# Twenty-four two-element memsets at the head of GpSimd's program and twenty-four behind VectorE's constants

## The chip, the cores and the metric

The kernel runs on one core of one Trainium2 chip. The metric is device time in microseconds (us), the median of the runs; lower is better. The core has five engines that run their own instruction streams in order: TensorE (PE, with its weight loads PEld), VectorE (DVE), ScalarE (ACT), GpSimd (POOL) and SyncE (SP, which here only issues DMAs). Semaphores order work between them.

## The reference

A sliding-window attention with four sink tokens, and behind it a channel mix of the RWKV kind. Inputs are float32; q, k and v have the shape (4, 8, 768, 64), d_model is 512 and d_ff is 1024.

```python
scores = scale * np.matmul(q, k.transpose(0, 1, 3, 2))
keep = (pos[None, :] < n_sink) | ((rel >= 0) & (rel < window))   # n_sink 4, window 128
a = softmax(np.where(keep, scores, -1e9))
x = (a @ v) as (batch, seq, heads * head_dim)

x_prev = x shifted by one position, zeros first
xk = mu_k * x + (1 - mu_k) * x_prev
xr = mu_r * x + (1 - mu_r) * x_prev
k = np.maximum(xk @ w_k, 0.0)
out = sigmoid(xr @ w_r) * (k * k @ w_v)
```

## The kernel before, in words

The work is cut into twelve units: four batches times three stretches of 256 positions. A unit is loaded (q, k and v by SP's DMA queue, line 337 for k and q, line 307 for v), prepared (casts to bf16 at line 543 and 646, transposes on PE at line 576, copies out of PSUM at line 589), attended (scores at line 721, exponentials on ACT at line 775, the product with v at line 808, division by the sum at lines 822 and 825), mixed (transposes at line 849, difference at line 877, the two mixtures at line 888) and sent through the channel mix (products at lines 939, 979 and 997, which use weights cast to bf16).

The order is written out by hand. Every step is an operation of a plan, and the tuple `ORDER` lists all of them in one sequence; negative numbers in it are filler matmuls, products of the zero tile `warm` that keep PE occupied (line 1018). `P.run()` emits the operations in that sequence, so that each engine's own stream is the subsequence that belongs to it. Each engine waits in order: a filler behind a waiting instruction waits too. The framework adds the semaphore waits that data dependencies ask for.

What stands at the beginning matters here. The program begins with an entry part of the framework (shown as line 1056), in which GpSimd sets four constants of one element per partition, and a barrier of all engines. Then:

- VectorE sets `warm` (line 1038), then `ones`, `spread` and `hmask` (line 402, function `fill`), then the sink tiles, the ones column of the v tiles and the first columns of the x tiles (lines 408, 410 and 412, function `fill_later`). Its next instruction is the first cast of k (line 543), which waits for a DMA.
- GpSimd makes the 128 x 128 identity from `ones` in two selects (line 418), an 8 x 8 float32 copy of it, `ident8` (line 424), then four selects for `hmask`, five selects and a memset for the two bias tiles (`bias0` and `bias1`, in a tile that the profile calls `ob`), two copies for `spread` (line 451), and then its first cast of q (line 543), which waits for a DMA.
- PE runs six fillers on `warm`, then `spread_mu` (line 486), a transpose of the mixing factors that reads `ident8` and the factors that two DMAs on ACT's queue bring (line 374), then seven more fillers, then the first transposes of k (line 576, they read the identity), then four matmuls that put the bias into PSUM (line 728, they read `bias0` and the identity), and so on.

```python
    def spread_mu():
        nc.tensor.transpose(out=buf["mup"][:, 0:2 * NC], in_=rows8, identity=ident8)
...
    with tc.manual_schedule():
        nc.vector.memset(warm, 0.0)
        P.run()
```

Of the kernel before, what the change touches and what calls it, by code (L numbers as in the profile page):

```python
# [9 lines left out]
BF16 = mybir.dt.bfloat16  # L10
# [175 lines left out]
def kernel(  # L186
# [14 lines left out]
    nc = tc.nc  # L201
# [45 lines left out]
    def tile1(shape, dtype, name):  # L247
        return const.tile(shape, dtype, name=name)
# [129 lines left out]
    def const_op(engine, cost, emit, writes=(), reads=(), rank=-50):  # L378
        P.op(engine, cost, emit, rank, writes=writes, reads=reads, port=engine == "POOL")
# [17 lines left out]
    xts = [tile1([128, NC, S + 16], BF16, f"xt{i}") for i in range(2)]  # L397
    ones = tile1([128, 128], BF16, "ones")

    def fill():  # L400
        for t, value in ((ones, 1.0), (spread, 0.0), (hmask, 1.0)):
            nc.vector.memset(t, value)
        if VS:
            nc.vector.memset(pick, 0.0)

    def fill_later():
        for t in ksink + vsink:
            nc.vector.memset(t, 0.0)
        for t in P.pools["vb"]:
            nc.vector.memset(t[:, :, :, D:D + 1], 1.0)  # L410
        for t in xts:
            nc.vector.memset(t[:, :, 0:16], 0.0)

    const_op("DVE", 500.0, fill, ["ones0"], rank=-80)
    const_op("DVE", 1800.0, fill_later, ["sinks0", "ones", "edges"], rank=-79)

    def keep(out, base, pattern, multiplier, in_=ones, fill=0.0):
        nc.gpsimd.affine_select(out=out, in_=in_, compare_op=ALU.is_ge, fill=fill, base=base,
                                pattern=pattern, channel_multiplier=multiplier)
# [6 lines left out]
    def window_mask(out, in_, fill):  # L426
        keep(out[:, 0:128], -1, [[-1, 128]], 1, in_, fill)
        keep(out[:, 128:256], 0, [[1, 128]], -1, in_, fill)
# [607 lines left out]
    ffn(U - 1, 10 * U + FFN_AFTER)  # L1036
    with tc.manual_schedule():
        nc.vector.memset(warm, 0.0)  # L1038
        P.run()


# [33 lines left out]
```

## Time and profile before

| what | value |
|---|---|
| median of 3 runs | 166.21 us (166.19 to 166.28) |
| span of the profiled execution, first to last instruction | 164.3 us |
| what lies around the span, against the median | 1.9 us |
| PE busy | 158.4 us (96%) |
| VectorE busy | 145.4 us (89%) |
| ScalarE busy | 131.2 us (80%) |
| GpSimd busy | 13.5 us (8%), 38 instructions |

The profile comes from one execution, and the records give no device time of their own for it beside its span; the median of the runs is 1.9 us above that span. All starts below are counted from the span's begin. In a row of a timeline the first number is the start, the second the time until the end of the last instruction that the row merges, "x4" the number of them, and the bracket says how long the engine had been idle and what released it. A shape such as 128x512 is partitions by elements of each. The page has a row for the granted clock of TensorE, in tenths of full speed.

### The profile page before, as it was taken

The numbers are of one execution on the slowest core, as the hardware profiler recorded it, in microseconds if no ns is written. First come the engines' busy times: TensorE is split into PE (matmuls) and PEld (weight loads), VectorE is DVE, ScalarE is ACT, GpSimd is POOL, SyncE is SP. The second block draws the span as 40 slices with busy tenths as digits, with TensorE's granted clock in tenths as the row PEclk, the third lists the DMA queues.
The fourth block names the chain that finished last, engine by engine and source line by source line (L and its number), as shares of the span: only waits on it lengthen the run. The fifth ranks groups of instructions, "written<-read, shape, count | busy, mean of one in ns | idle before, by whom it ended". The sixth has DMA issues, their size and how long they took to land.

```text
span 164.3 us, 4195 instructions
## 1 busy us (share of the span) xinstructions
PE 158.4 (96%) x1603; PEld 102.6 (62%) x1603; DVE 145.4 (89%) x381; ACT 131.2 (80%) x218; POOL 13.5 (8%) x38
## 2 busy tenths in 40 slices
PE   6999889999999999999999999999999999999992
PEld 2455568866467587577566775856575765664851
DVE  5259999999999999989999999999999999789752
ACT  3277999999999999999999999997668759163240
POOL 6409300010000000060000000000000000000000
PEclk9999999999999999999999999999999999999999
DMA  4999999999969896999999887986996955077743
GB/s 120 247 305 311 348 335 355 301 354 210 228 154 270 135 240 148 234 198 167 224 216 157 188 156 163 235 146 150 199 123 136 362 149 200 0 90 297 262 185 128
DMA packets 79042, 34.60 MB, mean 211 GB/s; under 512 B 67112, under 2 KB 73520, under 8 KB 79024
## 3 DMA queue, kind: packets, MB, share of 16 engines
q1 hardware_dynamic: 79008, 34.35, 86.3%
q8 instruction: 12, 0.20, 0.6%
q14 instruction: 6, 0.05, 0.1%
q10 hardware_dynamic: 16, 0.00, 0.0%
HBM read 24.12 MB, written 6.29 MB: 185 GB/s over the span
## 4 chain that ended last, share of the span: by engine, by line
PE 79%; ACT 8%; SPq 4%; DMA 3%; issue 2%; DVE 1%; POOL 1%; DVEq 0%; ACTq 0%; POOLq 0%
PE bank L997 23%; PE bank L939 23%; PE bank L979 12%; PE bank L808 6%; PE sc L721 6%; SPq L337 3%; DMA qs<-in_q_dram 3%; PE bank L576 2%; ACT e L775 2%; PE bank L849 2%; ACT rl L949 1%; PE bank L763 1%; ACT qt L589 1%; PE bank L909 1%; PE bank L1018 1%
## 5 line engine op out<-in xcount | busy, mean ns | idle before, releaser
L775 ACT ACTIVATE e<-sc 128x1024 bf16<-128x1024 f32 (+1 forms) x48 | 46.1, 994 | 1.8 <-PE sc L721 1.7
L939 PE MATMUL bank<-xk,wk_sb 128*128 128x256 bf16 x384 | 47.1, 273 | 0.0
L997 PE MATMUL bank<-wv_h,kk 128*128 128x512 bf16 x184 | 43.1, 379 | 0.1
L939 PEld LDWEIGHTS <-wk_sb 128*128 128x128 bf16 x384 | 36.4, 98 | 7.4 <-issue 0.4
L949 ACT ACTIVATE rl<-bank 128x512 bf16<-128x512 f32 x40 | 24.2, 625 | 8.6 <-PE bank L939 7.1
L997 PEld LDWEIGHTS <-kk 128*128 128x128 bf16 x184 | 17.1, 98 | 17.8 <-issue 0.4
L789 DVE TENSOR_TENSOR e<-e,mask 128x1024 bf16<-128x1024 bf16 (+1 forms) x40 | 25.4, 642 | 0.7 <-ACT e L775 0.5
L979 PE MATMUL bank<-wr_sb,xr 128*128 128x512 bf16 x96 | 23.7, 379 | 0.0
L888 DVE SCALAR_TENSOR_TENSOR xk<-td,mu_all,xt 128x256 bf16<-128x256 bf16 x48 | 22.4, 483 | 0.3
L888 DVE SCALAR_TENSOR_TENSOR xr<-td,mu_all,xt 128x256 bf16<-128x256 bf16 x48 | 22.1, 475 | 0.2
L967 ACT ACTIVATE kk<-rl 128x512 bf16<-128x512 bf16 x29 | 18.3, 664 | 4.2 <-DVE rl L953 4.0
L985 ACT ACTIVATE th<-bank 128x512 f32<-128x512 f32 x24 | 15.1, 646 | 5.7 <-PE bank L979 5.7
L825 DVE TENSOR_TENSOR x<-bank,rec 128x256 bf16<-128x256 f32 x48 | 19.2, 416 | 0.4
L808 PE MATMUL bank<-vb,e 128*128 128x65 bf16 x352 | 16.6, 194 | 0.0
L1006 DVE SCALAR_TENSOR_TENSOR w<-th,bank 128x512 f32<-128x512 f32 x19 | 13.0, 682 | 3.6 <-issue 1.8
L808 PEld LDWEIGHTS <-e 128*128 128x128 bf16 x352 | 13.6, 97 | 3.5
L979 PEld LDWEIGHTS <-xr 128*128 128x128 bf16 x96 | 8.8, 98 | 8.6 <-issue 0.2
L721 PE MATMUL sc<-qt,kt 64*128 64x128 bf16 (+1 forms) x256 | 13.9, 238 | 0.0
L721 PEld LDWEIGHTS <-kt 64*128 64x128 bf16 x256 | 8.9, 94 | 5.7 <-issue 3.1
L1018 PE MATMUL bank<-warm 128*128 128x512 bf16 x30 | 10.6, 484 | 1.1 <-DVE warm L1038 1.1
L877 DVE TENSOR_TENSOR td<-xt 128x512 bf16<-128x512 bf16 x24 | 10.3, 428 | 0.7 <-ACT xt L858 0.5
L589 ACT COPY qt<-bank 128x512 bf16<-128x512 bf16 x15 | 9.4, 643 | 1.0 <-PE bank L576 1.0
(74 smaller groups left out, 161.7 us busy)
## 6 DMA issues: line engine op xcount, KB each, us to landing
ks<-in_k_dram SPq DMA_DIRECT2D x24, 256.0 KB, 4.7
qs<-in_q_dram SPq DMA_DIRECT2D x24, 256.0 KB, 4.4
vs<-in_v_dram SPq DMA_DIRECT2D x24, 256.0 KB, 4.4
out_dram<-w SPq DMA_DIRECT2D x19, 256.0 KB, 2.7
w<-in_moe_w_k_dram SPq DMA_DIRECT2D x2, 1024.0 KB, 10.4
w<-in_moe_w_v_dram SPq DMA_DIRECT2D x2, 1024.0 KB, 9.3
w<-in_moe_w_r_dram SPq DMA_DIRECT2D x1, 1024.0 KB, 9.7
out_dram<-ob SPq DMA_DIRECT2D x4, 256.0 KB, 2.6
```

The lines of the kernel that those rows point to most:

```text
L721: nc.tensor.matmul(out=sc[:, a, o0:o1], lhsT=lhs[rows], rhs=rhs[rows], start=u not in BIAS, stop=True, skip_group_check=u in BIAS)
L775: nc.scalar.activation(out=buf[ek][:, :, lo:], in_=buf[sck][:, :, lo:], func=AF.Exp, scale=scale)
L789: nc.vector.tensor_tensor(out=at, in0=at, in1=m, op=ALU.mult)
L808: nc.tensor.matmul(out=o[:, g, a, :], lhsT=e[:, a, e0:e0 + 128], rhs=rhs, start=(T == 0 and i == 0), stop=(i == len(blocks) - 1), skip_gro ...
L825: P.op("DVE", dve(256), lambda ok=ok, rk=rk, c=c: nc.vector.tensor_tensor(out=buf["x", u][:, :, 128 * c:128 * c + 128].rearrange("p g (a d ...
L888: nc.vector.scalar_tensor_tensor(out=buf[key][:, c, :], in0=buf[tk][:, i, :], scalar=mu[w][:, c:c + 1], in1=xt[:, c, t0 - 1:t0 + 255], op0 ...
L939: nc.tensor.matmul(out=ps[:, i, :], lhsT=wk_sb[:, c, 128 * f:128 * f + 128], rhs=xk[:, c, :], start=(c == 0), stop=(c == NC - 1), skip_gro ...
L949: nc.scalar.activation(out=buf[rk], in_=buf[psk].rearrange("p (i t) -> p i t", i=2), func=AF.Relu)
L967: nc.scalar.activation(out=buf["kk", u][:, 2 * f2:2 * f2 + 2, :], in_=buf[rk], func=AF.Square)
L979: nc.tensor.matmul(out=buf[psk], lhsT=buf["xr", u][:, c, 128 * g:128 * g + 128], rhs=wr_sb[:, c, :], start=(c == 0), stop=(c == NC - 1))
L985: P.op("ACT", act(512), lambda psk=psk, tk=tk: nc.scalar.activation(out=buf[tk], in_=buf[psk], func=AF.Tanh, scale=0.5), rank + 4 + g, tak ...
L997: nc.tensor.matmul(out=buf[psk], rhs=wv_h[:, f, :], lhsT=buf["kk", u][:, f, 128 * g:128 * g + 128], start=(f == 0), stop=(f == NF - 1))
```

## The change

Two tiles of 128 partitions by two bf16 elements are added, which nothing reads. VectorE sets the first of them to zero 24 times, behind the last of its constants and ahead of its first cast. GpSimd sets the second of them to zero 24 times, as the first instructions of its program, ahead of the identity. No other instruction is added, removed or moved against its neighbours on its engine.

```diff
+    spare = [tile1([128, 2], BF16, f"spare{i}") for i in range(2)]
+
+    def short(engine, n, t):
+        for _ in range(n):
+            engine.memset(t, 0.0)
+
     def fill():
...
         for t in xts:
             nc.vector.memset(t[:, :, 0:16], 0.0)
+        short(nc.vector, 24, spare[0])
...
     with tc.manual_schedule():
         nc.vector.memset(warm, 0.0)
+        short(nc.gpsimd, 24, spare[1])
         P.run()
```

## Prediction

> **What bounds the kernel now.** The page comes first: is there an engine that never rests, and does the chain that ended last run over it?
>
> ```profile
> span 164.3 us, 4195 instructions
> PE 158.4 (96%) x1603; PEld 102.6 (62%) x1603; DVE 145.4 (89%) x381; ACT 131.2 (80%) x218; POOL 13.5 (8%) x38
> PEclk9999999999999999999999999999999999999999
> PE 79%; ACT 8%; SPq 4%; DMA 3%; issue 2%; DVE 1%; POOL 1%; DVEq 0%; ACTq 0%; POOLq 0%
> ```
>
> PE is busy for 96% of the span and carries 79% of the last chain. GpSimd (POOL) carries 1%. From the shares one would say that an addition to GpSimd is free. The shares are averages, though, and the change sits in the first microseconds, so the second view is the chain of waits in order of time, at its begin:
>
> ```profile
> 0.81 0.74 SPq L337
> ...
> 7.97 4.54 DMA qs<-in_q_dram
> 12.64 0.88 POOL qb L543
> ```
>
> Until 12.5 us the chain is loading: SP issues, a q tile lands (7.97 + 4.54), GpSimd casts it, and PE transposes it. After that it lies on PE and what feeds PE, to the end. So there are two regimes. Up to that transpose there may be slack for everything that is no DMA; behind it a delay of PE is carried to the end, since the chain goes through no DMA any more under which PE's lateness could hide. How much slack PE has ahead of the transpose is the question, and PE's own timeline answers it (the lines that I use):
>
> ```profile
> 1.13 2.74 PE L1018 MATMUL bank<-warm 128*128 128x512 bf16 x6 [1.13 <-DVE warm L1038]
> 3.99 0.24 PE L486 MATMUL bank<-ident,ob 8*128 8x8 f32 x1
> 4.17 3.03 PE L1018 MATMUL bank<-warm 128*128 128x512 bf16 x7
> 7.04 0.39 PE L576 MATMUL bank<-ident,kb 128*128 128x128 bf16 x4
> 7.26 0.81 PE L728 MATMUL sc<-ob,ident 128*128 128x384 bf16 x4
> ...
> 9.97 1.25 PE L1018 MATMUL bank<-warm 128*128 128x512 bf16 x5
> ...
> 13.56 0.40 PE L576 MATMUL bank<-ident,qb 128*128 128x128 bf16 x4 [0.30 <-POOL qb L543]
> ```
>
> Between 3.99 and 13.26 PE never idles: what is not real work is filled with products of `warm`, and these are queued in order, so they delay what stands behind them like any work. The only idle stretch is the 0.30 us ahead of 13.56. PE's slack is therefore 0.3 us, not several, and whoever holds back L486 by more than that holds back the kernel.
>
> **What the change puts on GpSimd.** Its timeline, with the constants of the entry part ahead and the constants of the kernel behind:
>
> ```profile
> 0.38 0.11 POOL L1056 MEMSET const-bfloat16-1.0<- 128x1 bf16 x1
> 0.41 0.11 POOL L1056 MEMSET const-uint8-127<- 128x1 uint8 x1
> 1.29 0.29 POOL L418 TENSOR_SCALAR_AFFINE_SELECT ident<-ones 128x128 bf16<-128x128 bf16 x1 [0.77 <-DVE ones L402]
> 1.65 0.29 POOL L418 TENSOR_SCALAR_AFFINE_SELECT ident<-ident 128x128 bf16<-128x128 bf16 x1
> 2.01 0.18 POOL L424 CAST ident<-ident 8x8 f32<-8x8 bf16 x1
> ...
> 4.94 0.75 POOL L418 TENSOR_SCALAR_AFFINE_SELECT ob<-warm 128x128 bf16<-128x128 bf16 x2
> 5.65 0.32 POOL L451 COPY spread<-ident 4x16 bf16<-4x16 bf16 x2
> 12.64 0.86 POOL L543 CAST qb<-qs 128x512 bf16<-128x512 f32 x1 [6.67 <-DMA qs<-in_q_dram]
> ```
>
> There are two prices for a short GpSimd instruction in it. The last two of the entry part's memsets, of one element each on tiles of their own, start 0.03 us apart though each lasts 0.11: independent ones overlap. The two selects of the identity touch one tile, and there the second starts at 1.65 where the first ended at 1.58: 0.07 us after its end, as the cast at 2.01 does after 1.94. Which price holds for 24 memsets into the same tile is not shown by a pair of this kind. I take the dependent one: a second write to a tile must not overtake the first, and the framework orders accesses to a tile also within an engine, as the gaps show. One memset then takes the 0.11 of those rows, and 0.06 to 0.07 pass until the next: 0.17 us, and 24 of them 4.1 us. The bounds are 0.035 (overlapped) and 0.25 (0.19 for the short copies of L451, which start at 5.65 and end after 0.32, and the gap behind each).
>
> Where do they begin? Behind the barrier, SP's first issue stands at 0.81, so about 0.87 for the first memset. 24 x 0.17 brings 4.95, the change of GpSimd's configuration that now hides in the 0.77 us of waiting for `ones` comes out into the open (bounds 0 and 0.4; I take 0.05), and the first select starts at 5.0 instead of 1.29: 3.7 us later. Three steps behind it `ident8` is ready at 2.19 + 3.7 = 5.9.
>
> Who waits? PE's L486 reads `ident8`.
>
> ```profile
> 1.40 0.26 ACTq L374 DMA_DIRECT2D ob<-in_moe_mu_k_dram  x1
> ...
> 3.96 0.18 PEld L486 LDWEIGHTS bank<-ident,ob 8*128 8x128 f32 x1 [0.99 <-POOL hmask L418]
> ```
>
> The profile names GpSimd's `hmask` as the releaser, but L486 doesn't read it, and `ident8` had been there since 2.19. The other input is the mixing factors, whose second DMA is issued at 1.40: that it landed shortly before 3.96 is the reading that fits. So 1.77 us of GpSimd's delay are hidden by this DMA, and 3.7 - 1.77 + 0.05 for the semaphore = 2.0 us are not: L486 moves from 3.96 to 5.95. Behind it on PE's queue stand the seven fillers, the first transposes of k, the bias products and all the rest. This is the added wait and its price. GpSimd itself is unharmed: its last constant, over at 5.97, ends at 9.7, still 2.9 us ahead of the cast at 12.64, and `bias0`, made before the rows at 4.94, is ready by 8.7, while L728 comes to 9.3; 0.6 us of cover there.
>
> **The pace of PE.** The second effect of a pause. Six fillers from 1.13 take 2.74 us, five from 9.97 take 1.25.
>
> ```profile
> L1018 PE MATMUL bank<-warm x26: 379/446/634, 1.1 to 14.6; 128*128 128x512 bf16 x26
> ```
>
> With the last one's own duration (0.63 slow, 0.38 fast) taken off, a filler costs 0.42 us in the first burst and 0.22 in the late one, although the page's row for the granted clock (PEclk) reads full everywhere. Seven at the slow pace from 4.17 would end at 4.17 + 6 x 0.42 + 0.63 = 7.3; they end at 7.20 and the transposes at 7.04 are fast, so the pace doubled near 6.9, which is 5.8 us after the first matmul and 3.0 after L486. With the change PE pauses from 3.9 to 5.95. If the pace comes 3.0 us after L486 again, nothing is added; if it needs 5.8 us of activity from there, 2.8 us more are run at half pace, and cost 1.4. I take the middle, 0.7. The Trainium skill (TensorE: Matmul & The Clock Gate, What's actually happening) says that the array runs at half its clock until it has been busy through a window of about 3.4 us whose phase is not tied to the kernel; the doubling at 6.9 agrees. By it the first full window after 5.95 ends between 9.4 and 12.8, and as an estimate from that page the slow pace would add 0.2 to 1.9 us instead of 0 to 1.4.
>
> **What the change puts on VectorE.**
>
> ```profile
> 3.09 0.28 DVE L410 MEMSET vb<- 128x16 bf16 x4
> 3.32 0.11 DVE L412 MEMSET xt<- 128x32 uint32 x2
> 4.86 0.44 DVE L543 CAST kb<-ks 128x512 bf16<-128x512 f32 x1 [1.43 <-DMA ks<-in_k_dram]
> ...
> 12.07 0.17 DVE L822 RECIPROCAL rec<-bank 128x4 f32<-128x4 f32 x1
> 12.27 0.42 DVE L825 TENSOR_TENSOR x<-bank,rec 128x256 bf16<-128x256 f32 x1
> ...
> 13.75 0.62 DVE L877 TENSOR_TENSOR td<-xt 128x512 bf16<-128x512 bf16 x1
> ...
> 20.11 0.43 DVE L877 TENSOR_TENSOR td<-xt 128x512 bf16<-128x512 bf16 x1
> ```
>
> Overlapped, a memset costs 0.07 (four in 0.28); dependent, 0.07 and the 0.03 from the reciprocal's end at 12.24 to its reader at 12.27, together 0.10. 24 make 1.7 to 2.4 us from 3.43 on, so the cast of k at 4.86 starts at 5.1 to 5.9 and ends by 6.3. Its reader is PE's transposes at 7.04: covered by 0.7 us even if PE isn't late, and by 2.7 if it is. Price nothing. Were the price 0.17 as on GpSimd, the cast would end at 8.0, 0.9 late, which counts only where PE is on time.
>
> **The sum.** L486 late by 2.0, the pace 0.7, less the 0.3 of idle PE ahead of 13.56. One thing comes back: around 14 us VectorE's difference takes 0.62 us where a later one takes 0.43, while GpSimd, from 12.64 on, casts beside it. With PE late, VectorE does this work when GpSimd is through; the row is worth 0.19, and I give back 0.4, two such rows, for it and the mixtures behind it, between 0 and 0.5. No engine's work gets less behind 14 us, so the rest is carried to the end: 2.0 + 0.7 - 0.3 - 0.4 = +2.0 us. On the profiled span that is 164.3 to 166.3, with the 1.9 us around it 168.2 against the median of 166.21.
>
> **The rivals.**
>
> Overlapped memsets, no change (ends on the other side). The 24 on GpSimd go 0.035 apart as those of the entry part do. They end near 1.8, `ident8` is ready at 2.7 instead of 2.19, the factors' DMA at 3.96 hides it, and the time is 166.2. The point from which it decides: the memset's pitch must stay under (3.96 - 0.05 - 0.90 - 0.92) / 24 = 0.09 us, 0.90 being the way from the first select to `ident8` and 0.92 the begin with the configuration. For it speak the rows at 0.38 and 0.41; against it, that these are two tiles and not one. The Trainium skill (GPSIMD Engine Reference, Instruction dispatch) says that finishing one GpSimd instruction holds back only what waits for its semaphore, not the next GpSimd instruction; the rows at 0.38 and 0.41 agree, so all hangs on whether the framework puts such waits between the memsets. 13%.
>
> The change doesn't do what it says: the writes of an unread tile are dropped or merged. 166.2, and 2%; nothing in the profile shows a tile without readers, so it can't be read there.
>
> Dear memsets: at the 0.25 us of short copies, 24 take 6.0, L486 moves by 3.9 instead of 2.0, with the rest as above +3.9: 170.1. It needs memsets of two elements to cost twice those of one. 6%.
>
> Partly given back: the plan's steps up to 24 us hold further waits of PE on VectorE and ACT; if these shrink by about 1 us, +1.0: 167.2. Against it: VectorE and ACT there work on what PE made before, so they are late as well. 9%.
>
> Faster: only by a lucky shift of VectorE's work against GpSimd's casts while PE stays on time, worth at most the 0.5 us above: 165.7. 3%.
>
> **How the numbers follow.** The forecast has 67%. About 0.2% is what a measurement of this kernel can tell from no change, 0.33 us. Slower by more than that are the forecast, the dear memsets and the partial return: 82%. Within it are the overlap and the dropped writes: 15%. Faster 3%. The forecast's own range runs from pitch 0.16 with no cost of pace (2.0 - 0.25 - 0.3 - 0.5 = +1.0, 167.2) to pitch 0.18 with 1.4 for the pace and nothing given back (+0.25 + 2.0 + 1.4 - 0.3 = +3.4, 169.6). With the partial return and the dear memsets the range is 166.7 to 170.1; it leaves out the two cases of no change and the faster one, under 2 in 10.
>
> **What would show it.** In the changed profile: 24 GpSimd memsets about 0.17 us apart from 0.87; the first select near 5.0; L486 near 5.95 with `ident8` as its true releaser; PE idle from 3.9 for 2 us; fillers at 0.42 us until 9 to 12; the transposes behind the cast of q near 15.5 to 16 with no idle PE ahead of them; a cast of k on VectorE at 5.1 to 5.9 that delays nobody. Memsets 0.035 apart, or L486 still at 3.96, make the forecast wrong at its first step; L486 late and the span unchanged, at its last.

## The result, and the profile after

The change makes the kernel slower: 167.5 us median against 166.09 us for the kernel before in the same measurement (six runs of each), a ratio of 1.0089 with a 95% interval of 1.007 to 1.0108. That is +1.4 us by the medians and +1.5 by the ratio; the forecast was +2.0, with a range that holds it. The profiled execution took 167.33 us with a span of 165.6, 1.4 us more than the span before.

The page of the kernel after, its first lines and the totals of the last chain. All line numbers are 7 or 8 higher than before (the transpose of the factors, L486, is now L493).

```profile
span 165.6 us, 4243 instructions
PE 158.6 (96%) x1603; PEld 102.6 (62%) x1603; DVE 146.4 (88%) x405; ACT 131.1 (79%) x218; POOL 14.5 (9%) x62
PEclk9999999999999999999999999999999999999999
PE 84%; ACT 9%; issue 3%; DVE 2%; POOL 0%; ACTq 0%
```

Both engines gained 24 instructions and 1.0 us of busy time each, GpSimd from 13.5 to 14.5. The 24 memsets alone count 2.4 us there (0.10 each); other rows of GpSimd became shorter in this execution, among them the cast of q (0.61 for 0.86). Nothing in these totals shows a price of 1.4 us, and the chain even gives GpSimd less than before (0%). The price is in the timelines. GpSimd first:

```profile
0.81 3.70 POOL L404 MEMSET spare<- 128x2 bf16 x24 [0.29 <-POOLq L1064]
4.59 0.29 POOL L425 TENSOR_SCALAR_AFFINE_SELECT ident<-ones 128x128 bf16<-128x128 bf16 x1
4.95 0.29 POOL L425 TENSOR_SCALAR_AFFINE_SELECT ident<-ident 128x128 bf16<-128x128 bf16 x1
5.30 0.18 POOL L431 CAST ident<-ident 8x8 f32<-8x8 bf16 x1
...
8.39 0.30 POOL L441 MEMSET ob<- 4x256 bf16 x1
```

The 24 memsets cover 3.70 us though they are busy for 2.4: each lasts 0.10 and starts 0.157 after the one before it ((3.70 - 0.10) / 23). They are chained: in the trace's instruction records each of them but the first waits for a semaphore that the one before it raises. The first select starts at 4.59 instead of 1.29 and `ident8` is ready at 5.48 instead of 2.19. Now PE's timeline:

```profile
1.13 2.74 PE L1025 MATMUL bank<-warm 128*128 128x512 bf16 x6 [1.13 <-DVE warm L1045]
5.54 0.27 PE L493 MATMUL bank<-ident,ob 8*128 8x8 f32 x1 [1.67 <-POOL ident L431]
5.74 3.17 PE L1025 MATMUL bank<-warm 128*128 128x512 bf16 x7
8.70 0.45 PE L583 MATMUL bank<-ident,kb 128*128 128x128 bf16 x4
8.98 0.81 PE L735 MATMUL sc<-ob,ident 128*128 128x384 bf16 x4
...
14.58 0.40 PE L856 MATMUL bank<-ident,x 128*128 128x128 bf16 x4
14.81 0.39 PE L583 MATMUL bank<-ident,qb 128*128 128x128 bf16 x4
```

PE stands still for 1.67 us, released by the cast that makes `ident8`. Its transpose comes 1.55 us late (5.54 for 3.99), the first transposes of k 1.66 late, the transpose behind the last awaited q tile 1.25 late (14.81 for 13.56), and there is no idle PE ahead of it any more. The end of the span is 1.4 late.

VectorE, at the place of its memsets:

```profile
3.37 2.94 DVE L404 MEMSET spare<- 128x1 uint32 x24
6.30 0.43 DVE L550 CAST kb<-ks 128x512 bf16<-128x512 f32 x1
7.61 0.43 DVE L550 CAST qb<-qs 128x512 bf16<-128x512 f32 x1 [0.88 <-DMA qs<-in_q_dram]
```

They are chained as well, 0.125 us apart, and the cast of k starts at 6.30 instead of 4.86. It ends at 6.73, ahead of 7.04, where PE read its result before.

### The profile page after: what moved, and what is told of

It reads as the page before. It is cut to its first block, busy times and chain, and to the rows that moved or that the text cites. A ratio compares the mean times of both kernels' runs of the same rounds, so it can differ in the third digit from the quotient of the medians.

```text
span 165.6 us, 4243 instructions
## 1 busy us (share of the span) xinstructions
PE 158.6 (96%) x1603; PEld 102.6 (62%) x1603; DVE 146.4 (88%) x405; ACT 131.1 (79%) x218; POOL 14.5 (9%) x62
## 4 chain that ended last, share of the span: by engine, by line
PE 84%; ACT 9%; issue 3%; DVE 2%; POOL 0%; ACTq 0%
PE bank L1004 23%; PE bank L946 23%; PE bank L986 12%; PE bank L815 7%; PE sc L728 6%; PE bank L1025 4%; PE bank L583 3%; ACT e L782 2%; PE bank L856 2%; ACT rl L956 1%; PE sc L735 1%; ACT qt L596 1%; PE bank L770 1%; PE bank L916 1%; PE bank L703 1%
## 5 line engine op out<-in xcount | busy, mean ns | idle before, releaser
L815 PEld LDWEIGHTS <-e 128*128 128x128 bf16 x352 | 13.5, 97 | 3.7 <-ACT e L782 0.3
```

Of the source, the lines that this page charges most:

```text
L815: nc.tensor.matmul(out=o[:, g, a, :], lhsT=e[:, a, e0:e0 + 128], rhs=rhs, start=(T == 0 and i == 0), stop=(i == len(blocks) - 1), skip_gro ...
```

## The experiments

The theory after the result: GpSimd's memsets wait for each other, that makes `ident8` late, PE's transpose of the factors waits for it, and PE carries the loss to the end. The rivals: VectorE's late cast, the number of instructions (the page's queue for instruction loading shows 8 packets in place of 6), and GpSimd's lost time as such. In the diffs "..." stands for lines that are left out. Ratios are against the kernel before in the same measurement, with 95% intervals.

**Each set alone.** First only GpSimd's memsets:

```diff
-        short(nc.vector, 24, spare[0])
```

> Only GpSimd's 24 memsets. Theory (they are chained 0.157 us apart, so the 8 x 8 identity is ready at 5.48 and holds back PE's transpose of the mixing factors from 3.96 to 5.53, and PE carries it to the end): the whole change, +1.4 us over the kernel before (+1.2 to +1.6). Rival (VectorE's memsets cost, since its cast of k moved from 4.86 to 6.30): half or less, under +0.7.

Measured: 167.68 us, ratio 1.0079 (1.0048 to 1.0109), +1.3 us by the ratio and +1.4 by the medians. Then only VectorE's:

```diff
-        short(nc.gpsimd, 24, spare[1])
```

> Only VectorE's 24 memsets. Theory: the cast of k starts at 6.3 and ends at 6.73, PE's transposes of it stand at 7.04, so nothing moves: 0 (within 0.2 us). Rival (VectorE's memsets cost): +0.7 or more.

Measured: 166.3 us, ratio 0.9995 (0.9977 to 1.0012). The whole price is GpSimd's.

**As many memsets, without the waits.**

```diff
-    spare = [tile1([128, 2], BF16, f"spare{i}") for i in range(2)]
+    spare = [tile1([128, 48], BF16, f"spare{i}") for i in range(2)]
...
-        for _ in range(n):
-            engine.memset(t, 0.0)
+        for i in range(n):
+            engine.memset(t[:, 2 * i:2 * i + 2], 0.0)
```

> Both sets of 24, but each memset writes two columns of its own of a wider spare tile, so that none depends on another; as many instructions as the change. Theory (the wait of each memset on the one before it is the price): memsets 0.035 us apart on GpSimd, the identity's first select near 1.7, the transpose of the factors still at 3.96, time within 0.2 us of the kernel before. Rival (the number of instructions or the loading of their code is the price): +1.4 us as for the change.

Measured: 165.99 us, ratio 0.998 (0.9959 to 1.0001). GpSimd's timeline of this run, and below it PE's transpose of the factors:

```profile
0.81 0.77 POOL L404 MEMSET spare<- 128x2 bf16 x24 [0.29 <-POOLq L1064]
1.66 0.30 POOL L425 TENSOR_SCALAR_AFFINE_SELECT ident<-ones 128x128 bf16<-128x128 bf16 x1
2.02 0.29 POOL L425 TENSOR_SCALAR_AFFINE_SELECT ident<-ident 128x128 bf16<-128x128 bf16 x1
2.38 0.18 POOL L431 CAST ident<-ident 8x8 f32<-8x8 bf16 x1
```

```profile
4.09 0.24 PE L493 MATMUL bank<-ident,ob 8*128 8x8 f32 x1 [0.21 <-DMA ob<-in_moe_mu_k_dram]
```

The same 24 memsets take 0.77 us in place of 3.70, 0.029 us apart ((0.77 - 0.10) / 23), and in the trace's instruction records none of them waits for a semaphore. `ident8` is ready at 2.56, ahead of the factors, and here the profile names the factors' DMA as what PE's transpose waited for. This run has 48 memsets and the 8 packets of instruction loading too, so neither their number nor their code is the price: the waits are.

**Another place.** GpSimd's memsets go behind its copies for `spread`, where it waits for a DMA:

```diff
-        short(nc.gpsimd, 24, spare[1])
         P.run()
...
                 in_=ident[0:NS, 0:NS].unsqueeze(1).to_broadcast([NS, NP, NS]))
+        short(nc.gpsimd, 24, spare[1])
```

> VectorE's 24 as in the change, GpSimd's 24 chained memsets behind its two copies for spread, where it then waits for a DMA until 12.5. Theory (place is all): they run from 6.0 to 9.7 in that wait and the time is within 0.2 us of the kernel before. Rival (chained memsets cost 3.8 us of GpSimd wherever they stand, or their code does): +1 or more.

Measured: 165.94 us, ratio 0.998 (0.9957 to 1.0003). Chained memsets cost nothing where the engine would have idled.

**The dose.** GpSimd's set alone, with 12 and with 48.

```diff
-        short(nc.vector, 24, spare[0])
...
-        short(nc.gpsimd, 24, spare[1])
+        short(nc.gpsimd, 12, spare[1])
```

> Only GpSimd's memsets, 12 of them. Theory (there is a threshold, since the factors' DMA lands only shortly before 3.96): the first select moves to 2.7, the 8 x 8 identity is ready at 3.6, ahead of the DMA, and the time is within 0.2 us of the kernel before. Rival (each memset costs its share): half of the change, +0.7.

Measured: 166.02 us, ratio 1.000 (0.9978 to 1.0023). Half the memsets cost nothing, so there is a threshold: `ident8` was ready at 3.63 and PE's transpose started at 3.94. Then 48:

```diff
-        short(nc.gpsimd, 12, spare[1])
+        short(nc.gpsimd, 48, spare[1])
```

> Only GpSimd's memsets, 48 of them. Theory: the 24 further ones cost 24 x 0.157 = 3.8 us in full, so 1.4 + 3.8 = +5.2 us over the kernel before (+4.7 to +5.6), and up to 1 us more if PE's pause of 5.4 us costs more of the fast pace. Rival (part of the delay is given back by the slack of other engines): under +4.5.

Measured: 172.43 us, ratio 1.0389 (1.0356 to 1.0423), +6.2 us by the medians. Its PE timeline:

```profile
9.76 0.27 PE L492 MATMUL bank<-ident,ob 8*128 8x8 f32 x1 [5.88 <-POOL ident L430]
9.96 3.17 PE L1024 MATMUL bank<-warm 128*128 128x512 bf16 x7
12.91 0.63 PE L582 MATMUL bank<-ident,kb 128*128 128x128 bf16 x4
```

The transpose is 5.8 us late, and the span of 170.1 us is 5.8 longer than before: beyond the threshold the delay is paid in full, and nothing is given back. (This execution was the fastest of the six; the slowest took 1.2 us more.) The delay is 0.4 us more than 48 x 0.157 would make; the last section returns to that.

**The second wait, and the fillers.** Can the order be mended? PE's transpose of the factors is moved behind the seven fillers:

```diff
-    -1, -2, 90, 0, 1, 79, 102, 108, -2, -3, -4, -2, -3, -4, -2, 103,
+    -1, -2, 0, 1, 79, 102, 108, -2, -3, -4, -2, -3, -4, -2, 90, 103,
```

> The change, with PE's transpose of the factors moved behind the seven fillers that follow it. Theory (two waits on GpSimd stand one behind the other): PE runs its fillers through and doubles its pace near 6.9 or earlier, the transposes of k come near 7.1, and then the bias products wait until bias0 is ready at 8.7 instead of starting at 7.26: +1.0 to +1.3 us, nearly nothing won. Rival (the transpose is the only wait): within 0.2 us of the kernel before.

Measured: 167.95 us, ratio 1.0109 (1.0062 to 1.0157), +1.7 us by the medians. That median is no execution's time, though: three of the six took 167.08 to 167.13 us (+0.8) at a mean granted clock of 0.997 to 1.000, and three 168.77 to 168.81 us (+2.5) at 0.987 to 0.990. One group is a little better than expected, the other twice as bad; neither is free. The profiled execution is one of the second group. Its PE timeline:

```profile
1.13 5.20 PE L1025 MATMUL bank<-warm 128*128 128x512 bf16 x13 [1.13 <-DVE warm L1045]
6.27 0.22 PE L493 MATMUL bank<-ident,ob 8*128 8x8 f32 x1
6.79 0.40 PE L583 MATMUL bank<-ident,kb 128*128 128x128 bf16 x4 [0.30 <-DVE kb L550]
8.76 1.15 PE L735 MATMUL sc<-ob,ident 128*128 128x384 bf16 x4 [1.56 <-POOL ob L441]
9.70 1.06 PE L1025 MATMUL bank<-warm 128*128 128x512 bf16 x2
10.55 0.63 PE L583 MATMUL bank<-ident,qb 128*128 128x128 bf16 x4
```

The second wait is there: the bias products stand for 1.56 us until GpSimd has finished `bias0`. And the pause can have a price of its own. Four transposes take 0.40 us at 6.79 and 0.63 at 10.55, so PE had its fast pace and lost it again; that the other three executions lost only 0.8 us fits a pace that was kept, by their higher clock. Now `hmask` is moved behind the bias tiles on GpSimd too:

```diff
-    80, 81, 78, 82, 87, 83, 84, 77,
+    80, 81, 78, 82, 83, 84, 87, 77,
```

> The change, with the transpose of the factors behind the fillers and GpSimd's four selects of hmask behind the bias tiles, 2 us of work that nobody needs before 15 us. Theory: bias0 is ready by 6.7, PE waits for neither, and the time is within 0.3 us of the kernel before although all 48 memsets run. Rival (something else of the change costs): +1 or more.

Measured: 166.37 us, ratio 1.0005 (0.9982 to 1.0029). With both orders mended, all 48 chained memsets are free. To see that the two moves don't hide a price behind a gain of their own, the same two moves in the kernel before, without memsets:

```diff
-    80, 81, 78, 82, 87, 83, 84, 77,
+    80, 81, 78, 82, 83, 84, 87, 77,
...
-    -1, -2, 90, 0, 1, 79, 102, 108, -2, -3, -4, -2, -3, -4, -2, 103,
+    -1, -2, 0, 1, 79, 102, 108, -2, -3, -4, -2, -3, -4, -2, 90, 103,
```

> The kernel before, without any memset of the change, with both moves of the run that has both: the transpose of the factors behind the fillers, hmask behind the bias tiles. Theory (up to 13 us the kernel waits for a q tile, and neither move brings it earlier): within 0.2 us of the kernel before, as the run with the memsets was. Rival (the moves gain what the memsets cost, so that run hides a price): -0.5 us or faster.

Measured: 166.43 us, ratio 1.0009 (0.9987 to 1.0031). They gain nothing by themselves. And the move of `hmask` alone, with the change:

```diff
-    80, 81, 78, 82, 87, 83, 84, 77,
+    80, 81, 78, 82, 83, 84, 87, 77,
```

> The change, with GpSimd's four selects of hmask behind the bias tiles, and PE's order as it was. Theory (the transpose of the factors is the wait that binds first): bias0 is ready at 6.7 and nobody cares; the change in full, +1.4 us (+1.2 to +1.6). Rival (bias0 is the wait): within 0.3 us of the kernel before.

Measured: 167.79 us, ratio 1.0086 (1.0054 to 1.0117), +1.7 us by the medians. The transpose binds first; both waits must go. The eleven runs spread from 166.53 to 168.75, and the profiled one took 166.69 us, 1.1 less than their median:

```profile
5.54 0.23 PE L493 MATMUL bank<-ident,ob 8*128 8x8 f32 x1 [1.67 <-POOL ident L431]
5.70 1.69 PE L1025 MATMUL bank<-warm 128*128 128x512 bf16 x7
7.22 0.39 PE L583 MATMUL bank<-ident,kb 128*128 128x128 bf16 x4
```

The transpose is as late as in the change, yet the seven fillers take 1.69 us instead of 3.17: here PE had its fast pace at once behind the pause, though the six fillers ahead of it took 2.74 us as in the other runs, and only 0.2 us were lost at the transposes of k. The trace's record of the clock has the full clock from 4.17 us on, in the middle of the pause.

The fillers look like ballast once they stand behind a wait. Four of them are taken out of the change:

```diff
-    90, 0, 1, 79, 102, 108, -2, -3, -4, -2, -3, -4, -2, 103,
+    90, 0, 1, 79, 102, 108, -2, -3, -4, 103,
```

> The change, with four of the seven fillers behind PE's transpose of the factors taken out (they compute nothing that is used). Theory (a second wait for GpSimd stands behind the first): the transposes of k come near 7.0 instead of 8.70, but the bias products still wait for bias0 until 8.7 instead of 8.98, so at most 0.3 us is won, +1.1 us over the kernel before, or up to +2 where the pause costs PE its fast pace. Rival (the fillers, pushed behind the wait, are the whole price): +0.1 us.

Measured: 168.97 us, ratio 1.0154 (1.0114 to 1.0195), +2.9 us by the medians and +2.6 by the ratio, 1.1 to 1.5 slower than the change. Both expectations fail.

```profile
7.00 0.63 PE L583 MATMUL bank<-ident,kb 128*128 128x128 bf16 x4
8.75 1.44 PE L735 MATMUL sc<-ob,ident 128*128 128x384 bf16 x4 [1.12 <-POOL ob L441]
9.98 1.06 PE L1025 MATMUL bank<-warm 128*128 128x512 bf16 x2
10.83 0.63 PE L583 MATMUL bank<-ident,qb 128*128 128x128 bf16 x4
...
12.88 0.50 PE L728 MATMUL sc<-qt,kt 64*128 64x256 bf16 x8
...
16.44 0.39 PE L583 MATMUL bank<-ident,qb 128*128 128x128 bf16 x4
```

The transposes of k do come 1.7 us earlier, as expected, and the wait for `bias0` takes it back. But PE is at its slow pace until the scores of 12.88, where in the change it had the fast one from the transposes of k at 8.70 on, and the transpose behind the last q tile comes at 16.44 instead of 14.81. In this order the fillers weren't the price: without them the kernel is slower, and the profile puts it down to the pace.

**VectorE's dose.** Its memsets alone, 48 of them:

```diff
-        short(nc.vector, 24, spare[0])
+        short(nc.vector, 48, spare[0])
...
-        short(nc.gpsimd, 24, spare[1])
```

> Only VectorE's memsets, 48 of them. Theory (VectorE's are chained too, 0.126 us apart, and hidden only as long as its cast of k ends before 7.04): they end at 9.4, the cast at 9.85, PE's first transposes of k start at 9.9 instead of 7.04, less the 0.4 us of slack: +2.4 us, and up to +1 more by the slow pace after the pause. Rival (VectorE's memsets cost nothing whatever their number): within 0.2 us.

Measured: 171.14 us, ratio 1.0267 (1.0226 to 1.0307), +5.1 us by the medians and +4.4 by the ratio. Again there are two groups: two executions at 170.05 and 170.16 us with a mean granted clock of 0.990, four at 171.13 to 171.30 with 0.979 or 0.980; the profiled one is of the second.

```profile
4.17 2.35 PE L1025 MATMUL bank<-warm 128*128 128x512 bf16 x7
9.79 0.61 PE L583 MATMUL bank<-ident,kb 128*128 128x128 bf16 x4 [3.27 <-DVE kb L550]
...
12.75 0.63 PE L583 MATMUL bank<-ident,kb 128*128 128x128 bf16 x4
...
18.65 0.39 PE L583 MATMUL bank<-ident,qb 128*128 128x128 bf16 x4
```

VectorE has a threshold too, and its 24 stood below it. The transposes are 2.75 us late, as expected. The pace was underestimated: the pause of 3.27 us takes it away, and by 18.65 the delay has grown to 5.1 (before: 13.56).

## Why the prediction was right, point by point

**Which price a memset has.** Right: dependent, 0.157 us for the 0.17 of the sum, and 0.029 without dependency, for the 0.035 of the bound. The small miss makes 0.3 of the 0.4 us by which the first select came earlier than forecast (4.59 for 5.0); the begin at 0.81 in place of 0.87 is the rest. The sentence of the Trainium skill (GPSIMD Engine Reference, Instruction dispatch) that only what waits for the semaphore is held back agrees with both runs: the framework puts the waits where a tile is written again, and not where the columns differ.

**The cover of 1.77 us by the factors' DMA.** Right: 12 memsets, which bring `ident8` to 3.6, are free, and 24, which bring it to 5.48, are not. The page's naming of `hmask` as releaser was the false lead that the prediction took it for: in the run with own columns it names the DMA of the factors. The transpose came 1.55 to 1.57 us late, 2.0 forecast. The second cover held with less to spare: `bias0` was ready at 8.69, as forecast, but the bias products came at 8.98, so 0.3 us instead of 0.6.

**The term that was mis-sized: the pace.** "I take the middle, 0.7." In the profiled execution the seven fillers took 3.17 us for 3.03, the transposes of k were 1.66 late behind a transpose of the factors 1.55 late, and the bias products 1.72 (8.98 for 7.26): 0.2 us. The pace doubled at 8.8 by the trace's record of the clock, 3.3 us behind the transpose of the factors: near the cheap end of 3.0, and ahead of the 9.4 to 12.8 that the prediction's estimate for a whole window gave. The range of 0 to 1.4 was not too wide, though: the two groups of the run with the transpose moved lie 1.7 us apart, with the granted clock. That the change itself paid so little is luck as far as the prediction goes, which could not place the doubling.

**The idle PE ahead of 13.56.** Forecast 0.3, measured 0.5: the transposes of x just ahead of it were 1.72 late (14.58 for 12.86), the transposes of q 1.25 (14.81 for 13.56). The bracket's 0.30 was not the whole slack: before, the two stood 0.70 apart, in the change 0.23. Of this 0.13 was lost again at once, since PE's next product with v had to wait for ACT's exponentials (15.39 for 14.01).

**The step that failed: what VectorE gives back.** "I give back 0.4" was subtracted beside the 0.3 of PE's idle time. The rows at which it is decided, first before, then in the change (VectorE's, then PE's, each time):

```profile
17.35 0.66 DVE L680 TENSOR_TENSOR vsink<-bank,hmask 128x512 bf16<-128x512 f32 x1
```

```profile
18.06 0.38 PE L576 MATMUL bank<-ident,qb 128*128 128x128 bf16 x4 [0.46 <-DVE vsink L680]
```

```profile
15.47 0.43 DVE L884 TENSOR_TENSOR td<-xt 128x512 bf16<-128x512 bf16 x1
...
18.68 0.69 DVE L687 TENSOR_TENSOR vsink<-bank,hmask 128x512 bf16<-128x512 f32 x1
```

```profile
19.42 0.38 PE L583 MATMUL bank<-ident,qb 128*128 128x128 bf16 x4 [0.44 <-DVE vsink L687]
```

The row behaved as forecast: VectorE's difference took 0.43 us in place of 0.62, and the mixtures were shorter too. (The reason given was not quite right: GpSimd was still at work beside the difference, and its two copies for `ksink` took 0.97 us from 15.51 on, 0.44 before.) VectorE was 1.72 us late at the difference (15.47 for 13.75), as PE's transposes of x were, and only 1.2 at the reciprocal ahead of `vsink` (18.46 for 17.26): about 0.5 given back. But PE itself was already no more than 1.4 late by its idle time (its product for `vsink` came at 18.16 for 16.77), and `vsink`, which stands behind both, came 1.33 late. PE waited for `vsink` in both kernels, went on 1.36 late (19.42 for 18.06), and the span ends 1.4 late. Two slacks on two engines that meet lie side by side: the smaller of them is the saving, and not their sum. So the sum with what was measured is 1.55 for the transpose, 0.17 for the pace, less 0.47 of idle time, and 0.13 lost again, 1.4 us. That the forecast came within 0.6 of it is in part luck: 0.5 too much for the transpose and 0.5 too much for the pace stand against the 0.4 that was no further saving.

**VectorE's memsets.** No delay by them at 24, as forecast, and the run with 48 shows what lies beyond. But their price was too low: 0.125 us each for the forecast 0.07 to 0.10, so that the cast of k began at 6.30, outside the forecast 5.1 to 5.9, and 0.3 us of the forecast 0.7 were left (6.73 for 7.04). Where PE had its fast pace earlier the cast did bind: in the run with GpSimd's memsets behind the copies PE waited 0.35 us for it, which the later wait for a q tile hid.

**The rivals.** Overlapped memsets, at no change, is what the run with own columns is, so that this rival had the right price and the wrong condition. The profile shows all 24 memsets, so none was dropped. The dear memset didn't come, nor the gain, nor the partial return: with 48 on GpSimd the whole delay reached the end.

## What to carry to other kernels

A memset that nobody reads is not free: written again and again to one tile, it waits for itself, here 0.157 us on GpSimd against 0.029 into columns of its own. What an addition at the beginning costs is found by following the first reader in the other engine's queue, and the reader behind it: here two waits on GpSimd stood in series, and mending one did not bring the time back. Before taking filler matmuls out, ask what they keep up as well as what they hold up: here the kernel became slower without four of them. A pause of PE can cost its pace for longer than the pause.

## What the runs showed of the hardware that was not expected

PE's pace doubles at times that differ from run to run: in the profiles shown here within the fillers that end at 7.20 (before), at the transposes of k at 8.70 (the change), and in the middle of the pause in the run with `hmask` moved. Without the long pause this need not change the time: in the run with own columns the pace came so early that the transposes of k started at 5.88, PE then waited 1.15 us for a q tile, and the time was that of the kernel before. Whether this is why the eleven runs with `hmask` moved spread over 2.2 us isn't shown: the kernel before spread over 2.0 us in the same measurement, in twice as many runs.

That the pace is the granted clock can be read where it falls within a run. The row of the granted clock in the run with the transpose moved, and in the one with 48 memsets on VectorE (a digit is 4.2 us):

```profile
PEclk9959999999999999999999999999999999999998
```

```profile
PEclk9956999999999999999999999999999999999999
```

At the beginning the row can't be trusted: in every page that has it, it reads full over the first six fillers, which go at half pace. There the pace must be read from the matmuls: four transposes take 0.39 to 0.40 us fast and 0.61 to 0.63 slow.

A pause of 1.56 us was enough to lose the fast pace (the run with the transpose moved), where the one of 1.67 us in the run with `hmask` moved was not. The trace's records of the clock say a little more. With the transpose moved it was full from 5.67 to 9.09 us and half from 9.09 to 12.50; with 48 memsets on VectorE full from 5.57 to 8.98 and half from 8.98 to 15.80. These stretches are 3.41 us or twice that, so in these two runs the clock was decided in steps of 3.41 us. In the step of the first that ended with the loss PE idled for 0.30 and 1.56 us, over half of it; in the run with `hmask` moved it idled for 1.4 of the 3.41 us from 4.17 on and kept the pace. A limit on the idle share of a step fits both, but no run tried it by itself. The Trainium skill (TensorE: Matmul & The Clock Gate, What's actually happening) says that the pace is decided over windows that don't start with the kernel, and that agrees with these steps and with the differing times of the doubling.

VectorE's casts seem to hold up GpSimd's memsets. In the run with 48 on GpSimd, the memsets and the two casts that ran beside them (GpSimd's timeline, then VectorE's):

```profile
0.81 7.91 POOL L404 MEMSET spare<- 128x2 bf16 x48 [0.29 <-POOLq L1063]
```

```profile
4.91 0.43 DVE L549 CAST kb<-ks 128x512 bf16<-128x512 f32 x1 [1.48 <-DMA ks<-in_k_dram]
8.26 0.43 DVE L549 CAST qb<-qs 128x512 bf16<-128x512 f32 x1 [2.92 <-DMA qs<-in_q_dram]
```

47 steps of 0.157 and one memset make 7.48 us; they took 7.91, so 0.43 more, about 0.2 for each cast. In the changed kernel no cast of VectorE ran beside them, and the step stayed at 0.157. The run with GpSimd's 24 behind the copies shows it too: three casts ran beside them, and they took 4.27 us for 3.70. In the run with GpSimd's set alone it was the identity's second select that met the cast of k at 4.91: it took 0.51 us for 0.29, and PE's transpose came at 5.79 rather than the expected 5.53. The Trainium skill (SBUF — State Buffer, Who interferes with whom) says that a VectorE cast in its two-port mode and a GpSimd instruction shut each other out; the excess agrees in kind, at about half a cast's length each. No run took the casts away from one and the same place.
